# Mirrored score blocks: how they are stored and read back, and when the first expert units' rows are multiplied

## The chip, the cores and the metric

The kernel runs on one core of one Trainium2 chip. The metric is the device time of one execution in microseconds (us). A timed comparison of this kernel can tell a difference of about 0.2% (10 us) from no change.

## The reference, cut to what matters

Eight batches of 3072 tokens go through an attention without softmax, then each token through one of eight experts, then through one dense MLP.

```python
scores = (1 / S) * z @ z.T              # per batch, S = 3072, d_qk = 64: a symmetric matrix
attn   = maximum(scores, 0) ** 2        # symmetric too
x      = u * (attn @ v)                 # v: (3072, 256)
idx    = argmax(norm(x) @ norm(expert_emb).T / tau);  gate = softmax(...)[idx]
x      = gate * (relu(x @ w1[idx]) @ w2[idx])          # 256 -> 1024 -> 256
out    = elu(x @ w_in) @ w_out                         # 256 -> 2048 -> 256
```

All matmuls run in a split form: a factor is cut into a rounded part (hi) and the rest (lo), and hi·hi, hi·lo and lo·hi are summed, three matmuls for one.

## The kernel before

**Attention.** A batch has six chunks `c` of 512 query columns, and each chunk has twelve steps `m`, of 256 key rows each; `k = m // 2` is the 512-row key block. 8 x 6 x 12 = 576 steps make the attention stage. A step has a score part (four matmuls `pss<-zp,zk`, `pss<-zq,zk`) and, two steps later, an accumulating part (`psa<-hi,v`, `psa<-lo,v`, twelve matmuls). ScalarE (ACT) applies ReLU and square, and ACT or VectorE (DVE) make hi and lo.

Since the score matrix is symmetric, block (c, k) with k > c is computed once. In a step that computes it (a calc step), DVE transposes the two halves into a tile `mt` (`mir_tr`), and `mir_put` stores the 1 MB block in the DRAM buffer `mir[b, c, k]`. When the later chunk comes to it (a held step, `m < 2c`), it has no score matmuls: `mir_get` loads a tile `mr` for each step, `mir_g` and `mir_d` make hi and lo of it. Chunk 0 has no held step, chunk 5 has ten of twelve (`order_of` interleaves held and calc steps). A held step is 12 matmuls long and a calc step 16.

**Behind a chunk** `evac_ops` multiplies the sum with u, transposes it (`xt`) and stores it in the DRAM buffer `xr`. Behind each pair of chunks `pair_ops` loads the rows back (`x<-xr`, function `get`), ACT squares them with a row sum (line 617, `sq`), and `route_ops` computes gates and positions; POOL scatters token numbers into `tok`, eight scatters per pair, each behind the one before.

**Experts and MLP.** After the attention, units follow: A (512 rows of one expert), B (256 rows), M and D (MLP on 512 rows). For A and B, POOL gathers token numbers (`ids`), rows (`rows<-xr,ids`) and weights (`wst`); DVE multiplies the rows by their gate (line 1013's `gates`), SP stores them in `xg` (`put`) and loads them back in transposed order (`xt<-xg`, `get`).

**Order of the work.** All instructions are issued in program order on each engine, and this order is written out by hand: `at(n, fn)` hangs a piece of work on step n, `spread` shares pieces over a range of steps by planned loads of ACT and DVE. SP issues nearly all plain DMAs, in order, and waits in order: a DMA whose data or buffer isn't ready holds up all DMAs behind it. POOL does the same for gathers and scatters.

**Buffers.** Nearly all SBUF tiles come from one pool of 4 KB-per-partition slots (tag `g`, `NSLOT` = 45); `mt` and the gathered `rows` share a second pool (tag `wide`, `NWIDE` = 2). A new tile waits for the last user of the slot that it gets.

Steps that the change touches, with n the step of use: `mir_get` at n - `AHEAD` (line 1344); `mir_put` two steps after the second half (line 1353); for a pair that ends at step w, `get` at w + 3 and `sq` from w + `EV` + 3 (lines 1462 and 1465), the routing from w + `EV` + 9; for the first two expert units (units 0 and 1, at steps 576 and 580) gathers at n - 32 and n - 27, gates and `put` at n - 25 and n - 20, read-back at n - 15 and n - 10 (lines 1513 to 1543).

Of the kernel before, what the change touches and what calls it, by code (L numbers as in the profile page):

```python
# [7 lines left out]
F32 = mybir.dt.float32  # L8
F32R = mybir.dt.float32r
# [6 lines left out]

LAG = 2
RL = 5
EV = 4
NSLOT = 45  # L20
NWIDE = 2
AHEAD = 8


def ceil_div(a, b):
# [4 lines left out]
def attn_moe_mlp(ctx, tc, zT, zK, uT, v, emb, embT, tau, wp, w_in, w_out, out):  # L30
# [25 lines left out]
    XW = D + 64  # L56
# [8 lines left out]
    mir = {(b, c, k): dr.tile([128, 2048], F32, name="mir")  # L65
           for b in range(B) for c in range(NC) for k in range(c + 1, NC)}
# [3 lines left out]
    def again(tag):  # L70
        q = fixed[tag]
        q.append(q.pop(0))
        return q[-1]

    def slot(name, dt=F32, shape=(2, 512)):
        if fixed:
            w = 1
            for s_ in shape:
                w *= s_
            t = again("gr" if dt == F32R else "g")[:, :w]  # L80
            if len(shape) == 1:
                return t
            names = "abcd"[:len(shape)]
            return t.rearrange("p (%s) -> p %s" % (" ".join(names), " ".join(names)), **dict(zip(names[1:], shape[1:])))
        return sb.tile([128] + list(shape), dt, name=name, tag="g", bufs=NSLOT)

    def rslot(name):
        return slot(name, F32R)

    def wide(name, shape):  # L90
        if fixed:
            return again("wide")
        return sb.tile([128] + shape, F32, name=name, tag="wide", bufs=NWIDE)

# [16 lines left out]
    vec, act, pool, pe, sp = nc.vector, nc.scalar, nc.gpsimd, nc.tensor, nc.sync  # L111
# [46 lines left out]
    def at(n, fn, s=0):  # L158
        tasks[n][s].append(fn)
# [187 lines left out]
    P, PK, Q, V, XS, UT, AC, HL, PS, MT = {}, {}, {}, {}, {}, {}, {}, {}, {}, {}  # L347
# [124 lines left out]
    def mir_tr(C, m):  # L472
        k, s_ = divmod(m, 2)

        def fn():
            if s_ == 0:
                MT[C, k] = wide("mt", [8, 2, 2, 2, 32])
            vec.transpose(out=MT[C, k][:, :, s_], in_=MT.pop((C, k, s_)).rearrange("p j (x q r) -> p x q j r", q=2, r=32))
        return fn

    def mir_put(C, k):
        b, c = divmod(C, NC)

        def fn():
            sp.dma_start(mir[b, c, k], MT.pop((C, k)).rearrange("p x s q j r -> p (x s q j r)"))
        return fn

    def mir_get(C, m):
        b, c = divmod(C, NC)
        k, s_ = divmod(m, 2)  # L490

        def fn():
            t = HL[C, m] = slot("mr", F32, (4, 256))
            src = mir[b, k, c].rearrange("(i r) f -> r i f", r=32)
            for q in range(4):
                o = (q * 2 + s_) * 256
                sp.dma_start(t[q * 32:(q + 1) * 32], src[:, :, o:o + 256])
        return fn

    def x8(t):  # L500
        return t.rearrange("p j (x y) -> p j x y", y=64)

    def mir_g(C, m, n):
        r = HL[C, m].rearrange("p i (s j y) -> p j (i s) y", j=2, y=64)
        hi = rslot("hi")
        on_act = use_act(n, 1.15)
        if on_act:
            cp(x8(hi), r)
        HL[C, m] = hi, r, on_act
# [828 lines left out]
    for C in range(NCH):  # L1338
        c = C % NC
        for m in order_of(c):  # L1340
            n = len(steps)
            steps.append((held if m < 2 * c else calc, (C, m, n)))
            if m < 2 * c:
                at(n - AHEAD, mir_get(C, m))
                loadA[n] += 0.9
                loadD[n + 1] += 2.1
            else:
                loadA[n] += 2.0
                loadD[n + 1] += 1.2
                if m // 2 > c:  # L1350
                    at(n + 1, mir_tr(C, m), -1)
                    if m % 2:
                        at(n + 2, mir_put(C, m // 2))
                    loadD[n + 2] += 1.25

    units = [("A", 0)]
# [3 lines left out]
    j, t = NA1, 0  # L1360
# [68 lines left out]
    for b in range(B):  # L1429
        for c2 in range(1 if b == 0 else 0, NC // 2):  # L1430
            nat, swap = q_ops(b, c2)
            w = (b * NC + 2 * c2) * CS
            spread([nat], w - 10, w - 9, 0, 1.25)
            at(w - 8, swap)
    for b in range(1, B):
        n0 = (b - 1) * NC * CS
        half = NK // 8
        for k4 in range(half, NK // 4):
            vl, vo = v_ops(b, k4)
            w = n0 + 5 * CS + LAG + 2 * (k4 - half)  # L1440
            at(w - 5, vl)
            pairs(vo, w + 1, w + 3, 0.6, 0.52)
        for c2 in range(NC // 2):
            zl, zo = z_ops(b, c2)
            w = n0 + 4 + c2 * CS
            at(w, zl)
            pairs(zo, w + 4, w + 12, 1.13, 0.95)
        for k4 in range(half):
            vl, vo = v_ops(b, k4)
            w = n0 + CS + 2 + k4 * 8  # L1450
            at(w, vl)
            pairs(vo, w + 3, w + 9, 0.6, 0.52)
    for C in range(NCH):
        at(C * CS + 4, u_load(C))
        w = (C + 1) * CS + LAG
        mul, tr, put = evac_ops(C)
        spread([mul], w - 1, w, 1.2)
        spread([tr], w, w + 1, 1.25)
        at(w + 1, put)
        if C % 2:  # L1460
            dots, get, sq = pair_ops(chunk_group[C][0])
            at(w + 3, get)
            pre[w + 2].append(dots)
            loadD[w + 3] += 0.4
            spread(sq, w + EV + 3, w + EV + 8, 0, 0.55)
    route_end = {}
    late = []
    for g, cs in enumerate(groups):
        seg1, rank, seg2, sc, g5 = route_ops(g)
        w = (cs[-1] + 1) * CS + LAG + EV + 9  # L1470
        L = RL
# [17 lines left out]
    w = route_end[g1]  # L1489
    spread(plan1_ops(), w + 1, w + 6, 0.2)  # L1490
    p1 = w + 6
    w = route_end[len(groups) - 1]
# [6 lines left out]
    for i, (ld, ops) in enumerate(cb):  # L1499
        per = ceil_div(len(cb), B)  # L1500
        w = (i // per) * NC * CS + (i % per + 1) * 2 * CS // per - (CS if i >= per else 0)
# [3 lines left out]
    for un in units:  # L1505
        n = start[un]
        pv = prev[un]
        k = un[0]
        if k in "AB":
            lo_ = p1 if k == "A" and un[1] < NA1 else p2 + 1  # L1510
            wl, w1, w2 = weight_ops(un)
            ro, gates, put, get, h = rows_ops(un)
            w = max(n - (9 if k == "A" else 6), lo_)
            wr = max(n - 9, lo_)
            if un == units[0]:
                w, wr = n - 16, n - 32
                assert wr >= lo_
            if pv is not None and pv[0] == "B" == k:
                assert False
            if pv is not None and pv[0] == "M" and prev[pv] is not None and prev[pv][0] in "AB":  # L1520
                wr = max(n - 16, lo_)
            elif un == units[1]:
                wr = n - 27
            for o in ro:
                at(wr, o, 2)
            for o in wl:
                at(w, o, 2)
            if pv is not None and pv[0] in "AB":
                q = start[pv] + (2 if pv[0] == "A" else 1)
                o = (0, 1, 1, 2, 2, 3)  # L1530
            elif pv is not None:
                q = n - 3
                o = (0, 3, 3, 4, 5, 6)
            else:
                q = max(n - 7, lo_ + 3)
                o = (0, 1, 1, 2, 2, 3)
            for x, o_ in zip((w1[0], w1[1], w2[0], w2[1], w2[2], w2[3]), o):
                pairs(x, q + o_, q + o_ + 1, 0.6, 0.52)
            assert wr + 5 <= n - 4, (un, wr - n)
            early = un in units[:2]  # L1540
            wp_ = wr + 7 if early else max(wr + 3, n - 11)
            at(wp_, lambda gates=gates, put=put: ([g_() for g_ in gates], put()))
            at(wr + 17 if early else max(wr + 5, n - 9), get)
            tr, hl = xt_ops(un, h, XT, 4 if k == "A" else 2)
            spread([tr], n - 4, n - 3, 1.25)
            pre[n - 2] += hl
        elif k == "D":
            dl, do = d_prep(un)
            tr, hl = do
            at(n - 6, dl)  # L1550
            spread([tr], n - 4, n - 3, 1.25)
            pre[n - 2] += hl
        if k in "MD" and un != units[-1]:
            w = n + nst[k] + LAG - 1
            tr, put, get, *sc = out_ops(un)
            at(w, tr)
            at(w + 1, put)
            at(w + 2, get)
            spread(sc, w + 4, w + 6)
# [5 lines left out]

    def rest_tiles():
        with tc.If(count["v"] >= NBS):
            mine = {"g": [slot("rest", F32, (1024,)) for _ in range(5)],
                    "gr": [slot("restr", F32R, (1024,)) for _ in range(12)], "wide": [wide("rows", [4, XW])],
                    "s": [t_ps() for _ in range(2)], "acc": [t_acc()],  # L1570
                    "ids": [sb.tile([128, 4], I32, name="ids", tag="ids", bufs=8)]}
            fixed.update(mine)
            for t in range(NBS, NB):
                un = ("B", t)
                wl, w1, w2 = weight_ops(un)
                ro, gates, put, get, h = rows_ops(un)
                tr, hl = xt_ops(un, h, XT, 2)
                for o in ro + wl + gates + [put] + [o for x in w1 for o in x] + [get] + [o for x in w2 for o in x] + [tr] + hl:
                    o()
                for k in range(2):  # L1580
                    ab_h(un, k)
                    ab_d(un, k)
                for k in range(2):
                    b_acc(un, k)
            fixed.clear()
# [66 lines left out]
```

## Time and profile before

| | us |
|---|---|
| median of three runs | 5135.99 |
| lowest, highest | 5133.37, 5138.31 |
| the profiled execution | 5144.09 |
| its span, first to last instruction | 5142.3 |
| TensorE (PE) busy | 5100.9 (99%) |
| DVE busy | 3997.6 (78%) |
| ACT busy | 3463.5 (67%) |
| POOL busy | 1378.3 (27%) |
| the attention stage, until its last matmul | about 1947 |

The busy times are of one profiled execution. [...] A timeline gives each instruction with its start, its length, and in brackets how long its engine was idle before it and what released it; for SP and POOL it is their queues of DMA issues (SPq, POOLq). A wait for several things is put down to the one that came last by the profile, so the name of a DMA there can be that of another.

### The profile page before, as it was taken

Reading aid. Unit: us, or ns where it says so; the run is one execution under the profiler, and the core shown is the slowest. Engines: PE = TensorE matmul, PEld = TensorE weight load, DVE = VectorE, ACT = ScalarE, POOL = GpSimd, SP = SyncE. Lnnn points to the kernel's source line nnn. Section 1 sums busy time; section 2 is a strip of 40 time slices with the busy share of each in tenths; the row PEclk is TensorE's granted clock in tenths of the full one; section 3 lists DMA queues with packets and bytes.
Section 4 is the critical chain, followed back from the end, with each engine's and each line's share of the span. In section 5 each row is a group of like instructions: output and inputs, shape, how many; then the busy total and the mean of one; then the engine's idle time right before and its main releaser. Section 6 shows DMA issues by size and latency. Waiting matters only on the chain. (4 is left out here: it accounts for less than half of the span.)

```text
span 5142.3 us, 67066 instructions
## 1 busy us (share of the span) xinstructions
PE 5100.9 (99%) x23600; PEld 4234.4 (82%) x23600; DVE 3997.6 (78%) x5099; ACT 3463.5 (67%) x4101; POOL 1378.3 (27%) x1159
## 2 busy tenths in 40 slices
PE   9999999999999999999999999999999999999998
PEld 7788888888888778888888888888888888888887
DVE  8687878787787867887777777777777777777887
ACT  8586767667676755676666666666666666666776
POOL 0011111111111033424444444444333333331011
PEclk9999999999999999999999999999999999999999
DMA  8898879888979695324334334334233333331221
GB/s 248 220 234 194 231 187 233 197 219 211 217 194 223 184 230 154 83 60 124 104 109 127 98 105 130 100 107 131 80 84 84 84 84 84 84 85 50 46 50 38
DMA packets 713109, 708.32 MB, mean 138 GB/s; under 512 B 417916, under 2 KB 622975, under 8 KB 697408
## 3 DMA queue, kind: packets, MB, share of 16 engines
q1 hardware_dynamic: 639296, 500.07, 39.2%
q0 software_dynamic: 73472, 203.91, 13.0%
q8 instruction: 188, 3.08, 0.3%
q14 instruction: 153, 1.25, 0.1%
HBM read 440.20 MB, written 252.04 MB: 135 GB/s over the span
## 5 line engine op out<-in xcount | busy, mean ns | idle before, releaser
L135 PE MATMUL psa<-hi,v 128*128 128x512 f32 x4608 | 1149.6, 392 | 12.9 <-ACT hi L132 6.8
L135 PEld LDWEIGHTS psa<-hi,v 128*128 128x128 f32 x4608 | 864.1, 188 | 203.4 <-ACT hi L132 10.8
L135 PE MATMUL pss<-x2h,wi 128*128 128x512 f32 x2624 | 809.1, 390 | 0.0
L135 PE MATMUL psa<-hi,wo 128*128 128x512 f32 x3008 | 743.3, 389 | 0.0
L124 DVE SCALAR_TENSOR_TENSOR y<-e,y 128x1024 f32<-128x1024 f32 x384 | 467.5, 1218 | 308.7 <-ACT e L1182 307.0
L135 PEld LDWEIGHTS psa<-hi,wo 128*128 128x128 f32 x3008 | 564.7, 188 | 116.8
L1128 ACT ACTIVATE e<-pss 128x1024 f32<-128x1024 f32 x376 | 386.5, 1028 | 404.7 <-PE pss L135 376.7
L744 POOL DMA_INDIRECT tok<-idt,pi x192 | 229.1, 1193 | 1524.4 <-DMA tok<-idt,pi 781.8
L135 PE MATMUL psa<-lo,v 128*128 128x512 f32 x2304 | 617.6, 390 | 4.9 <-DVE lo L114 4.9
L449 ACT ACTIVATE r<-pss 128x1024 f32<-128x1024 f32 x336 | 344.3, 1025 | 393.5 <-PE pss L135 392.5
L1054 ACT ACTIVATE hi<-pss 128x1024 fp32r<-128x1024 f32 x198 | 203.8, 1029 | 571.9 <-PE pss L135 571.9
L135 PEld LDWEIGHTS pss<-x2h,wi 128*128 128x128 f32 x2624 | 490.6, 188 | 99.9
L135 PEld LDWEIGHTS psa<-lo,v 128*128 128x128 f32 x2304 | 433.1, 188 | 96.7 <-DVE lo L114 6.2
L135 PE MATMUL pss<-x2l,wi 128*128 128x512 f32 x1312 | 510.9, 389 | 0.0
L948 POOL DMA_INDIRECT out<-o,ids x192 | 242.4, 1262 | 981.2 <-DMA o<-orow 512.0
L114 DVE TENSOR_TENSOR y<-r,y 128x1024 f32<-128x1024 f32 x384 | 470.6, 1225 | 33.9 <-DVE y L124 1.4
L114 DVE TENSOR_TENSOR lo<-r,hi 128x1024 fp32r<-128x1024 f32 x336 | 408.9, 1217 | 109.3 <-ACT hi L132 106.3
L114 DVE TENSOR_TENSOR lo<-y,hi 128x1024 fp32r<-128x1024 f32 x384 | 470.6, 1226 | 21.6
L1182 ACT ACTIVATE e<-e 128x1024 f32<-128x1024 f32 x384 | 407.8, 1062 | 12.2
L1181 ACT ACTIVATE y<-e 128x1024 f32<-128x1024 f32 x384 | 407.2, 1061 | 9.5
L135 PE MATMUL pss<-xh,w 128*128 128x512 f32 x1312 | 404.7, 390 | 0.9 <-DVE w L114 0.6
L135 PE MATMUL psa<-hi,w 128*128 128x512 f32 x1312 | 405.1, 390 | 0.0
(181 smaller groups left out, 9100.9 us busy)
## 6 DMA issues: line engine op xcount, KB each, us to landing
mir<-mt SPq DMA_DIRECT2D x120, 1024.0 KB, 6.2
mr<-mir SPq DMA_DIRECT2D x960, 128.0 KB, 5.8
vs<-v SPq DMA_DIRECT2D x48, 512.0 KB, 8.4
u<-uT SPq DMA_DIRECT2D x48, 512.0 KB, 6.1
xr<-xt SPq DMA_DIRECT2D x192, 128.0 KB, 3.8
x<-xr SPq DMA_DIRECT2D x96, 256.0 KB, 9.5
orow<-xt SPq DMA_DIRECT2D x188, 128.0 KB, 2.6
o<-orow SPq DMA_DIRECT2D x47, 512.0 KB, 3.9
```

The source lines that it names most:

```text
L114: vec.tensor_tensor(out=o, in0=a, in1=b, op=op)
L124: vec.scalar_tensor_tensor(out=o, in0=a, scalar=s, in1=b, op0=op0, op1=op1)
L135: pe.matmul(o, lhsT=l, rhs=r, start=start, stop=stop, skip_group_check=True, tile_position=pos)
L449: act.activation(out=r, in_=p, func=AF.Relu, scale=1.0 / S)
L744: pool.indirect_dma_start(out=tok[:, :], out_offset=bass.IndirectOffsetOnAxis(ap=h["pi"][:, t:t + 1], axis=0), in_=K["idt"][:, gt:gt + 1], ...
L948: pool.indirect_dma_start(out=dst, out_offset=bass.IndirectOffsetOnAxis(ap=idx, axis=0), in_=src, in_offset=None, bounds_check=bound, oob_ ...
L1054: act.activation(out=hi, in_=p, func=AF.Relu)
L1128: act.activation(out=e, in_=p, func=AF.Relu, scale=-1.0)
L1181: act.activation(out=y, in_=e, func=AF.Tanh, scale=0.5)
L1182: act.activation(out=e, in_=e, func=AF.Exp, scale=-1.0)
```

## The change

The block in DRAM gets another layout. `mt` is arranged so that each partition holds four runs of 512 numbers (2 KB). `mir_put` stores it with four DMAs of 256 KB, each from 32 partitions, two at step n + 2 and two at n + 3, where one DMA of 8 KB runs from all 128 partitions did it. `mir_get` loads a whole block, both steps' halves, with one DMA of 8 KB per partition into all 128 partitions, where eight DMAs (four for each step) of 1 KB runs, each into 32 partitions, did it. The tile that it fills (`mw`) comes from the `wide` pool and no longer from the slots. It is issued five steps ahead of the block's first step, where each half was issued eight ahead.

The pool of slots shrinks from 45 to 39, `wide` grows from 2 to 5. The read-back of x behind a pair moves from w + 3 to w + 5, squares and routing three steps later. For expert units 0 and 1, gathers move to n - 26 and n - 20, gates and `put` to n - 16 and n - 12, the read-back to five steps behind them (n - 11 and n - 7). The number and sizes of matmuls, and what DVE and ACT compute, stay.

```diff
-EV = 4
-NSLOT = 45
-NWIDE = 2
-AHEAD = 8
+EV = 7
+NSLOT = 39
+NWIDE = 5
+AHEAD = 5
...
-                MT[C, k] = wide("mt", [8, 2, 2, 2, 32])
-            vec.transpose(out=MT[C, k][:, :, s_], in_=MT.pop((C, k, s_)).rearrange("p j (x q r) -> p x q j r", q=2, r=32))
+                MT[C, k] = wide("mt", [4, 2, 4, 2, 32])
+            vec.transpose(out=MT[C, k][:, :, s_], in_=MT.pop((C, k, s_)).rearrange("p j (x q r) -> p x q j r", q=4, r=32))
...
-    def mir_put(C, k):
+    def mir_put(C, k, part):
...
-            sp.dma_start(mir[b, c, k], MT.pop((C, k)).rearrange("p x s q j r -> p (x s q j r)"))
+            t = MT[C, k] if part == 0 else MT.pop((C, k))
+            dst = mir[b, c, k].rearrange("(x r) f -> r x f", r=32)
+            for i in (2 * part, 2 * part + 1):
+                sp.dma_start(dst[:, :, i * 512:(i + 1) * 512],
+                             t[i * 32:(i + 1) * 32].rearrange("p x s q j r -> p x (s q j r)"))
...
-    def mir_get(C, m):
+    def mir_get(C, k):
...
-            t = HL[C, m] = slot("mr", F32, (4, 256))
-            src = mir[b, k, c].rearrange("(i r) f -> r i f", r=32)
-            for q in range(4):
-                o = (q * 2 + s_) * 256
-                sp.dma_start(t[q * 32:(q + 1) * 32], src[:, :, o:o + 256])
+            t = wide("mw", [8, 2, 2, 64])
+            sp.dma_start(t.rearrange("p x s j y -> p (x s j y)"), mir[b, k, c])
+            for s_ in range(2):
+                HL[C, 2 * k + s_] = t[:, :, s_]
...
-        r = HL[C, m].rearrange("p i (s j y) -> p j (i s) y", j=2, y=64)
+        r = HL[C, m].rearrange("p x j y -> p j x y")
...
-                at(n - AHEAD, mir_get(C, m))
+                if m % 2 == 0:
+                    at(n - AHEAD, mir_get(C, m // 2))
...
-                        at(n + 2, mir_put(C, m // 2))
+                        at(n + 2, mir_put(C, m // 2, 0))
+                        at(n + 3, mir_put(C, m // 2, 1))
...
-            at(w + 3, get)
+            at(w + 5, get)
...
-                w, wr = n - 16, n - 32
+                w, wr = n - 16, n - 26
...
-                wr = n - 27
+                wr = n - 20
...
-            wp_ = wr + 7 if early else max(wr + 3, n - 11)
+            wp_ = n - (16 if un == units[0] else 12) if early else max(wr + 3, n - 11)
...
-            at(wr + 17 if early else max(wr + 5, n - 9), get)
+            at(wp_ + 5 if early else max(wr + 5, n - 9), get)
...
-            mine = {"g": [slot("rest", F32, (1024,)) for _ in range(5)],
-                    "gr": [slot("restr", F32R, (1024,)) for _ in range(12)], "wide": [wide("rows", [4, XW])],
+            mine = {"g": [slot("rest", F32, (1024,)) for _ in range(4)],
+                    "gr": [slot("restr", F32R, (1024,)) for _ in range(10)], "wide": [wide("rows", [4, XW])],
```

The last two lines belong to a branch for left-over tiles (`rest_tiles`), which these inputs don't take.

## Rows read from the trace of the kernel before

**Rows 1.** The page: busy time of each engine, instructions, issues of the mirrored blocks.
```profile
PE 5100.9 (99%) x23600; PEld 4234.4 (82%) x23600; DVE 3997.6 (78%) x5099; ACT 3463.5 (67%) x4101; POOL 1378.3 (27%) x1159
...
mir<-mt SPq DMA_DIRECT2D x120, 1024.0 KB, 6.2
mr<-mir SPq DMA_DIRECT2D x960, 128.0 KB, 5.8
```
**Rows 2.** View by windows: all stretches of the attention where TensorE loses time.
```profile
230.00:250.00 20.00, 15.96 (x65) 12.61 (x64) 9.04 (x15) 8.15 (x11) 0.00 (x0) 0.91 0.68 180
715.00:725.00 10.00, 8.52 (x38) 6.47 (x37) 4.01 (x6) 5.45 (x6) 0.00 (x0) 1.00 0.52 154
1670.00:1680.00 10.00, 8.23 (x38) 6.23 (x36) 2.84 (x5) 4.36 (x5) 0.00 (x0) 1.00 0.75 197
1835.00:1850.00 15.00, 11.49 (x45) 8.84 (x44) 11.21 (x20) 6.21 (x7) 7.38 (x7) 0.89 0.64 155
1858.00:1868.00 10.00, 8.60 (x37) 6.43 (x36) 9.53 (x23) 5.04 (x5) 7.87 (x8) 1.00 0.73 187
1890.00:1910.00 20.00, 14.65 (x57) 11.67 (x56) 7.12 (x7) 9.06 (x22) 0.00 (x0) 0.83 1.12 271
```
**Rows 3.** Timeline of ACT: two waits, in the first and the last batch.
```profile
236.61 1.06 ACT L132 ACTIVATE hi<-mr 128x1024 fp32r<-128x1024 f32 x1 [11.28 <-DMA xr<-xt]
...
1895.79 0.42 ACT L617 ACTIVATE x<-x 128x256 f32<-128x256 f32 x1 [12.12 <-DMA x<-xr]
```
**Rows 4.** Timeline of DVE: two waits in the last batch.
```profile
1836.89 1.25 DVE L478 STREAM_TRANSPOSE mt<-r 128x1024 f32<-128x1024 f32 x1 [5.21 <-DMA mir<-mt]
...
1857.21 0.35 DVE L118 TENSOR_SCALAR rows<-rows 128x256 f32<-128x256 f32 x1 [6.72 <-DMA rows<-xr,ids]
```
**Rows 5.** Timeline of SP's DMA queue, in the first and the last batch.
```profile
219.46 9.20 SPq L497 DMA_DIRECT2D mr<-mir  x8
...
1827.40 0.34 SPq L485 DMA_DIRECT2D mir<-mt  x1
```
**Rows 6.** Timeline of POOL: scatters of the last pair before unit 0, unit 0's gathers.
```profile
1783.68 1.28 POOL L744 DMA_INDIRECT tok<-idt,pi  x1 [40.18 <-DVE pi L716]
...
1842.68 1.06 POOL L943 DMA_INDIRECT ids<-tok,ixa  x1 [4.86 <-DMA tok<-idt,pi]
...
1855.78 1.00 POOL L943 DMA_INDIRECT rows<-xr,ids  x1 [0.30 <-issue]
```
**Rows 7.** View by windows: mr loads; an mt store; an xt store; an o load.
```profile
1101.50:1103.50 2.00, 2.00 (x11) 1.65 (x10) 2.00 (x3) 1.38 (x4) 0.00 (x0) 1.00 1.35 216
521.00:523.00 2.00, 2.00 (x11) 1.65 (x10) 2.00 (x3) 1.85 (x2) 1.67 (x1) 1.00 1.07 442
...
868.00:870.00 2.00, 2.00 (x11) 1.65 (x10) 2.00 (x2) 0.62 (x1) 1.14 (x2) 1.00 1.02 221
3196.50:3198.50 2.00, 2.00 (x12) 1.69 (x11) 1.43 (x3) 2.00 (x5) 0.00 (x0) 1.00 1.00 351
```
**Rows 8.** View by windows: chunks 1 and 5 of the second batch.
```profile
299.60:340.60 41.00, 41.00 (x184) 33.77 (x183) 38.05 (x67) 36.02 (x39) 4.95 (x5) 1.00 0.93 258
...
456.70:493.10 36.40, 36.40 (x163) 29.98 (x162) 26.32 (x51) 20.41 (x26) 4.07 (x4) 1.00 0.66 148
```
**Rows 9.** The tile `vs` (v as loaded), from 250 to 1800 us: landing of its loads.
```profile
DMA to landing us min/median/max: 7.9/8.4/8.9
```
**Rows 10.** The tile `wst`, from 2100 to 4800 us: landing of its gathers.
```profile
DMA to landing us min/median/max: 4.1/5.1/7.5
```
**Rows 11.** Timelines of POOL, DVE and ACT: a B unit's rows, gates and weights.
```profile
2550.17 1.72 POOL L943 DMA_INDIRECT rows<-xr,ids  x1 [0.30 <-issue]
...
2553.70 1.73 POOL L943 DMA_INDIRECT wst<-wp,wiB  x1 [0.30 <-DVE w L114]
...
2558.26 0.61 DVE L118 TENSOR_SCALAR rows<-rows 128x256 f32<-128x256 f32 x2
...
2576.68 1.66 ACT L132 ACTIVATE w<-wst 128x512 fp32r<-128x512 f32 x3
```

## The prediction before the run

> **What bounds the kernel now.** I read the page first: TensorE is busy 99% of the span [rows 1], so the kernel is a queue of matmuls and only stretches in which TensorE stands still can give anything. The change leaves every matmul in place, so the second view is the one by windows, searched for stretches in which TensorE's busy time is short of the window. In the attention stage there are six [rows 2]; idle time in them is 4.04, 1.48, 1.77, 3.51, 1.40 and 5.35 us, 17.6 us together. [...] Counted as lost clock that is 0.09 x 20 + 0.11 x 15 + 0.17 x 20 = 6.9 us, an upper bound since part of it falls into the idle time itself. So **at most 24.4 us (0.5%)** can be won; the first microseconds, the tail and the expert stage have losses that the change doesn't touch.
>
> The third view says what each stretch waited for. At 230, ACT wanted an `mr` tile for 11.28 us [rows 3], and its loads had been issued slowly, eight of them in 9.20 us [rows 5]: the loads of mirrored blocks had fallen behind. The name in the bracket is of another DMA. The stretches at 715 and 1670 look the same; all three lie in the last chunk of a batch, where ten of twelve steps read mirrored blocks. At 1835, DVE waited 5.21 us before a transposition into `mt` [rows 4]: one of the two `wide` buffers held unit 0's gathered rows, and the other was still being stored by the DMA issued at 1827.40 [rows 5]. At 1858, DVE stood 6.72 us before unit 0's gate products because the rows had not landed [rows 4]. At 1890, ACT stood 12.12 us before the squares of x [rows 3].
>
> **The change, part by part.**
>
> *Five `wide` buffers.* The 5.21 us wait needs both buffers taken. With at most three to four `mt` and `mw` tiles alive at once in a batch (a block is held about eight steps from its load to its last use, and one comes every 2.4 steps in chunk 5), the wait goes. In the last batch the rows of a unit make it five of five, so there SP may wait for the buffer of a `mir_get`, with u's and x's DMAs queued behind it; that stays inside the five steps of lead. Gain 3.51 + 1.65 = 5.2 us.
>
> *Gates of units 0 and 1 later.* DVE reached unit 0's gates at 1857.21 - 6.72 = 1850.5 [rows 4]; they move nine steps later, 9 x 3.0 us (a chunk of 36.4 us has twelve steps [rows 8]) = 27 us, less the 5.2 us just won: 1872. The rows depend on POOL, which was busy with eight scatters from 1783.68 until the gathers at 1842.68 [rows 6]. The routing comes three steps later, so this chain and the gathers behind it come up to 9 us later: the last rows, 1857.2 before, at 1866. The margin is 6 us. Gates and the `put` that waits for them on SP then hold up nobody. Unit 1 moves by eight steps and has the same margin or more; its read-back keeps three steps, 9 us, before it is transposed. Gain 1.4 us.
>
> *x later.* Squares move three steps, their load two, which alone is 3 us against a wait of 12.12. What matters more is SP's order: the load stood behind unit 0's `put`, itself waiting for the gates until 1857; now it stands ahead of that `put`. The routing that follows is late by 9 us, and only units 0 to 5 can feel that, through POOL. Gain 5.35 + 3.4 us at most; I take 7.5.
>
> *Mirrored blocks read whole.* Per block, eight loads into 32 partitions become one. Loads of `mr` move 216 GB/s, a DMA of 8 KB runs over 128 partitions 442 [rows 7]: 1 MB in 4.85 or 2.4 us. SP issues 120 loads, not 960 [rows 1], and the eight issues of 9.20 us become one like that of `mir<-mt`, 0.34 us [rows 5]. In chunk 5, with five blocks, that takes 12 us off DMA engines that are busy 0.66 x 36.4 = 24 us in a quiet batch [rows 8]. The lead shrinks from eight steps to five, 15 us in chunk 5; the 1 MB store took 6.2 us from issue to landing [rows 1], so some 9 us are to spare. Gain: 5.8 us at 230 and 3.2 at 715 and 1670, of which I take 7.5.
>
> *Stores from 32 partitions.* This is the price, and no row shows this form. Its bounds: 351 GB/s, the 1 KB loads into 128 partitions, so 3.0 us a block, or 216 to 221 GB/s [rows 7], so 4.8. The rows divide by partitions and not by length of run: with 1 KB runs it is 216 into 32 partitions and 351 into 128, and the `xr<-xt` store from 32 partitions has 221. I take 4.8: a store then costs 2.4 us more, as much as a read saves, and the DMA load of a batch stays what it was but moves from its last chunks to its first. In chunk 1, with some five blocks stored and one or two read, 0.93 x 41.0 = 38.1 us of DMA [rows 8] become 38.1 + 5 x 2.4 - 1.5 x 2.4 = 46.5, which is 5.5 us too much for 41.0; chunk 3 and later give it back. At the other bound it is 38.1 + 3 - 3.6 = 37.5 us. Queued behind are v (loaded three or more steps of 3.4 us ahead, landing in 8.4 us [rows 9]) and the reads themselves (five steps, 17 us). Five microseconds of lateness are covered for the reads, and for v by its first use, mostly five steps after its issue. I cost it at nothing.
>
> [...]
>
> *Six slots fewer.* In the attention this pays for `mr`, up to eight of which were alive by the order of the steps. In the expert stage, 3.2 ms, it is a loss. A step of the MLP takes five slots (`e`, `y`, `r`, `hi`, `lo`) and lasts 24 matmuls, some 5.4 us, so a slot comes free 6/5 of a step later, 6.5 us. POOL's weight gathers feel it first. Their lead is 2576.68 - 2553.70 = 23 us [rows 11] and they land in at most 7.5 [rows 10], so 9 us stay. Behind them on POOL wait the next rows, the tightest 2558.26 - 2550.17 = 8.1 us before their gates [rows 11]; 6.5 us later, with 1.72 of issue and about 4 to landing, DVE would wait some 4 us in a few of 17 B units. Bounds: nothing, or those 4 us in all 17 less about 2 us of DVE's lead each, 34 us. I take nothing: most units have more lead, and the slot used next is not always the last one freed.
>
> **Sum.** 5.2 + 1.4 + 7.5 + 7.5 = 21.6, say **21 us**. The profiled execution took 5144.09 us, so it would take 5123; the median lies 8.1 us (0.16%) under it, so the forecast is **5115 us** (0.4% faster). If everything in the six windows goes, it is 5112; the standstills of the timed runs may be shorter or longer than those profiled, hence down to 5106.
>
> **The rivals.**
>
> *Stores clog the first chunks (slower).* At 216 GB/s chunk 1 ends 5.5 us late. If v and the reads of chunk 2 then miss their steps, ACT, which works in order, stands before v's conversion, and TensorE behind it, in each of eight batches. Price: 5.5 us x 8 = 44 on top of the forecast: **5159**. For it: the 0.93 [rows 8]. Against it: DMA shares count overlapping packets, and x's load now comes behind v's. It decides once the lateness passes some 5 us.
>
> *Fewer slots delay POOL (no change).* The 34 us bound halved, 17 us, against 21 won: **5132**, within 0.2%.
>
> *The standstills only move (no change).* Five steps of lead instead of eight, with DMAs as late as 11 us at times [rows 3], let the reads come late elsewhere, and the hand-over to the experts waits for POOL's chain. Only the two `wide` and gate parts stay, 7 us: **5129**.
>
> **How the numbers follow.** Forecast 0.70, stores 0.10, slots 0.08, moved standstills 0.12. A comparison tells about 0.2% (10 us) from no change, so below 5125.7 is faster and above 5146 slower. Faster: 0.70 and a little of the slots' case, 0.72; slower: the stores' 0.10 and the slots' bad end, 0.12; the rest 0.16. The range 5106 to 5138 covers the forecast, both no-change cases and leaves out the stores' case and the ends. The forecast's own range is 5106 to 5125.
>
> **What would show it.** Right: windows at 230, 715, 1670, 1835, 1858 and 1890 full at clock 1.00; `mw` loads landing in about 6 us and some 9 us before use; stores of 256 KB moving near 217 GB/s; DMA share of chunk 5 lower and of chunk 1 higher. Wrong: ACT idle before `v` or `hi<-mw` in chunks 1 to 3, DVE idle before `rows` in the B units, or SP waiting for `wide` buffers so long that the next read is late.

## The result, and the profile after

The change made the kernel slower: 5200.93 us (median of four runs, 5199.93 to 5213.47) against 5134.68 for the kernel before beside it (5132.61 to 5138.31). The ratio is 1.0133, with a 95% interval of 1.0121 to 1.0145. The forecast was 5115, so it missed by 86 us and had the wrong sign.

The profiled execution of after has a span of 5211.7 us, 69.4 more than that of before (it is the longest of the four runs; the medians differ by 66.2). First I cut both spans where the attention stage ends, at the start of its last matmul `psa<-lo,v`. The stage ends at 1946.7 us before and at 1989.9 after, 43.2 later. The expert stage behind it takes 3195.6 and 3221.8 us, 26.2 more. So there are two losses, in two stages, and neither lies where the forecast had looked for one.

The answer to [rows 1], from the page of after. The four stores and the one load per block are there as written, and TensorE has lost a point of its share:

```profile
PE 5126.4 (98%) x23600; PEld 4240.6 (81%) x23600; DVE 3976.9 (76%) x5078; ACT 3481.8 (67%) x4122; POOL 1340.7 (26%) x1159
...
mir<-mt SPq DMA_DIRECT2D x480, 256.0 KB
mw<-mir SPq DMA_DIRECT2D x120, 1024.0 KB
```

The six windows of [rows 2], in the trace of after (busy time of PE, PEld, DVE, ACT and POOL with their counts, the clock granted to TensorE as a share of full speed, the mean busy share of the DMA engines, which is over 1 where packets overlap, and GB/s):

```profile
230.00:250.00 20.00, 13.96 (x58) 11.19 (x57) 7.58 (x18) 5.49 (x7) 4.12 (x5) 0.92 0.37 81
715.00:725.00 10.00, 10.00 (x46) 8.29 (x45) 8.77 (x14) 9.51 (x16) 0.98 (x1) 1.00 0.82 252
1670.00:1680.00 10.00, 10.00 (x56) 7.58 (x55) 8.79 (x20) 5.04 (x5) 0.00 (x0) 1.00 0.70 210
1835.00:1850.00 15.00, 15.00 (x79) 12.02 (x72) 14.17 (x28) 8.29 (x10) 1.04 (x1) 1.00 0.86 221
1858.00:1868.00 10.00, 10.00 (x46) 8.29 (x45) 5.62 (x15) 7.26 (x12) 1.50 (x1) 1.00 1.02 306
1890.00:1910.00 20.00, 16.01 (x67) 12.58 (x67) 10.74 (x23) 7.33 (x8) 7.94 (x8) 0.89 0.75 190
```

Four are full. The windows lie at the same times as before, while the same work comes later here, so it takes the list of PE's waits to say what is left. The first and the last window still have a hole, but the DMA engines are quieter there (0.37 where it was 0.68, 0.75 where it was 1.12). It is another hole, and the waits of PE up to 1950 us name it:

```profile
PE pss L135 <- DMA zq<-zp: 47.3, 13, 6.0
PE pss L135 <- ACT zk L132: 6.2, 1, 6.2
```

Thirteen times TensorE stood before a score matmul because its tile `zq` had not landed, 47.3 us in all; before, this line does not exist. `zq` is the copy of `zp` with its halves of 64 partitions exchanged. It is made by two DMAs on **POOL's** queue, hung on step w - 8, eight steps before a pair of chunks starts (`swap` in `q_ops`). One such place, first in PE's timeline, then by windows:

```profile
909.21 0.39 PE L135 MATMUL pss<-zp,zk 128*128 128x512 f32 x1
914.48 0.77 PE L135 MATMUL pss<-zq,zk 128*128 128x512 f32 x1 [4.88 <-DMA zq<-zp]
```

```profile
911.00:916.00 5.00, 1.52 (x5) 0.94 (x6) 0.00 (x0) 0.00 (x0) 0.00 (x0) 0.63 0.42 79
916.00:922.00 6.00, 6.00 (x23) 4.83 (x23) 1.77 (x3) 5.04 (x5) 0.00 (x0) 0.74 0.00 0
```

The second window is the price on top: after a standstill of 4.88 us TensorE runs on at a granted clock of 0.74 in this window. Taken apart by smaller windows it is 0.50 from 912.4 to 919.1 us and 1.00 from 919.2 on. What kept the copies is in POOL's timeline, here of after, then the same place of before, with PE's first matmul on that `zq` below it:

```profile
853.50 1.04 POOL L746 DMA_INDIRECT tok<-idt,pi  x1 [46.51 <-DVE sm L129]
862.37 1.01 POOL L746 DMA_INDIRECT tok<-idt,pi  x1 [7.83 <-DMA tok<-idt,pi]
...
904.22 0.98 POOL L746 DMA_INDIRECT tok<-idt,pi  x1 [6.97 <-DMA tok<-idt,pi]
905.19 0.59 POOL L409 DMA_DIRECT2D zq<-zp  x1
```

```profile
821.66 1.05 POOL L744 DMA_INDIRECT tok<-idt,pi  x1 [27.80 <-DVE pi L716]
...
868.86 0.98 POOL L744 DMA_INDIRECT tok<-idt,pi  x1 [2.77 <-DMA mr<-mir]
869.83 0.59 POOL L409 DMA_DIRECT2D zq<-zp  x1
```

```profile
895.51 0.39 PE L135 MATMUL pss<-zq,zk 128*128 128x512 f32 x1
```

Both queues are the same: eight scatters of a pair's token numbers, each waiting for the one before to land, and right behind the last one the copies. Before, they were issued at 869.83 and land in a median of 8.0 us, about 878; TensorE's first matmul on that `zq` started at 895.51, so some 17 us were to spare. After, the scatters start 31.8 us later than the 821.66 of before (13.9 us of it because the kernel was already that late), the copies leave at 905.19, and TensorE wants them at 909.4.

In the expert stage no single line is large. One place of it, after the change, on POOL, then ACT, then PE:

```profile
2580.64 0.98 POOL L950 DMA_INDIRECT dn<-xo,dpB  x1 [0.30 <-ACT y L1183]
2588.84 1.25 POOL L950 DMA_INDIRECT dnid<-ids,dpB  x1 [7.22 <-DMA dnid<-ids,dpB]
2590.39 1.03 POOL L950 DMA_INDIRECT dn<-xo,dpB  x1 [0.30 <-issue]
```

```profile
2599.57 1.06 ACT L1183 ACTIVATE y<-e 128x1024 f32<-128x1024 f32 x1 [6.16 <-DMA dn<-xo,dpB]
```

```profile
2602.68 0.73 PE L135 MATMUL pss<-x2h,wi 128*128 128x512 f32 x2 [2.18 <-ACT r L1115]
```

ACT computes `y` from its own `e`; it has no business with `dn<-xo`. It waits because the slot that its `y` gets was that of `xo`, and POOL's second scatter out of `xo` has just left. Behind `y` on ACT stands the ReLU `r` that empties TensorE's score buffer, and TensorE waits 2.18 us. With fewer slots in the ring, a new tile meets a user that isn't done. From 2100 to 3700 us ACT's `y` waits 51.5 us for such scatters, in 12 places; before, never.

### The profile page after: what moved, and what is told of

The parts are those of the page before. It is cut to its first block, busy times and chain, and to the rows that moved or that the text cites. A ratio compares the mean times of both kernels' runs of the same rounds, so it can differ in the third digit from the quotient of the medians.

```text
span 5211.7 us, 66339 instructions
## 1 busy us (share of the span) xinstructions
PE 5126.4 (98%) x23600; PEld 4240.6 (81%) x23600; DVE 3976.9 (76%) x5078; ACT 3481.8 (67%) x4122; POOL 1340.7 (26%) x1159
## 3 DMA queue, kind: packets, MB, share of 16 engines
q0 software_dynamic: 73472, 203.91, 12.7%
## 5 line engine op out<-in xcount | busy, mean ns | idle before, releaser
L135 PE MATMUL psa<-hi,v 128*128 128x512 f32 x4608 | 1157.3, 394 | 0.0
L135 PEld LDWEIGHTS psa<-hi,v 128*128 128x128 f32 x4608 | 869.9, 190 | 190.5 <-issue 6.2
L135 PE MATMUL pss<-x2h,wi 128*128 128x512 f32 x2624 | 811.3, 390 | 9.9 <-ACT r L1115 9.6
L135 PE MATMUL psa<-hi,wo 128*128 128x512 f32 x3008 | 744.5, 390 | 1.3 <-issue 0.5
L135 PEld LDWEIGHTS psa<-hi,wo 128*128 128x128 f32 x3008 | 563.5, 188 | 122.3 <-issue 4.2
L135 PE MATMUL psa<-lo,v 128*128 128x512 f32 x2304 | 617.6, 390 | 0.0
L135 PEld LDWEIGHTS pss<-x2h,wi 128*128 128x128 f32 x2624 | 490.2, 188 | 114.0 <-ACT r L1115 13.5
L135 PE MATMUL pss<-x2l,wi 128*128 128x512 f32 x1312 | 511.0, 389 | 0.0
L135 PEld LDWEIGHTS psa<-lo,v 128*128 128x128 f32 x2304 | 434.4, 189 | 91.6
L950 POOL DMA_INDIRECT out<-o,ids x192 | 231.3, 1205 | 906.3 <-DMA o<-orow 454.4
L1183 ACT ACTIVATE y<-e 128x1024 f32<-128x1024 f32 x384 | 407.4, 1061 | 83.8 <-DMA dn<-xo,dpB 51.5
L135 PE MATMUL pss<-xh,w 128*128 128x512 f32 x1312 | 408.5, 391 | 4.2 <-DVE w L114 2.2
L135 PE MATMUL psa<-hi,w 128*128 128x512 f32 x1312 | 404.9, 390 | 0.0
```

The costliest lines, as they stand in the source:

```text
L135: pe.matmul(o, lhsT=l, rhs=r, start=start, stop=stop, skip_group_check=True, tile_position=pos)
L950: pool.indirect_dma_start(out=dst, out_offset=bass.IndirectOffsetOnAxis(ap=idx, axis=0), in_=src, in_offset=None, bounds_check=bound, oob_ ...
L1183: act.activation(out=y, in_=e, func=AF.Tanh, scale=0.5)
```

## The experiments

Three theories had to be told apart. **Theory 1**: the routing three steps later puts the scatters ahead of the `zq` copies. **Theory 2**: 39 slots instead of 45 cost the expert stage its 26 us. Against them: the new mirror transfers make things late, or the first units' new steps do. **Theory 3**, on the gains: the parts of the change bring what the sum gave them. All runs, with the cut of the profiled span as above (the kernel before took 5134.6, 5136.8, 5136.8 and 5132.4 us beside the runs of e1 to e4, e5 to e8, e9 to e11 and e12):

| kernel | attention ends at | rest of the span | median us | ratio to before, 95% |
|---|---|---|---|---|
| before | 1946.7 | 3195.6 | 5134.68 | 1 |
| after | 1989.9 | 3221.8 | 5200.93 | 1.0121 to 1.0145 |
| e1 after, `zq` copies on SP | 1924.3 | 3216.7 | 5142.27 | 1.0004 to 1.0023 |
| e2 after, routing back | 1921.1 | 3221.1 | 5142.70 | 1.0002 to 1.0021 |
| e3 before, routing later | 2022.3 | 3193.4 | 5222.16 | 1.0153 to 1.0187 |
| e4 before, six slots held | 1942.7 | 3215.0 | 5159.49 | 1.0027 to 1.0055 |
| e5 e2 + `x2h`, `x2l` in `wide` | 1921.0 | 3222.3 | 5145.44 | 1.0008 to 1.0027 |
| e6 e5 + `xo` in `wide` | 1921.1 | 3222.4 | 5145.43 | 1.0008 to 1.0027 |
| e7 e2 + first gates back | 1922.1 | 3217.9 | 5145.49 | 1.0006 to 1.0025 |
| e8 before + later gates, x | 1971.7 | 3195.3 | 5162.89 | 1.0029 to 1.0063 |
| e9 e5, as two tiles | 1921.4 | 3222.4 | 5145.48 | 1.0007 to 1.0027 |
| e10 e3 + copies on SP | 1941.1 | 3192.5 | 5137.60 | 0.9992 to 1.0011 |
| e11 e2 + DMA tiles in `wide` | 1921.1 | 3195.0 | 5117.72 | 0.9948 to 0.9976 |
| e12 e2 + `xh`, `xl` in `wide` | 1921.1 | 3236.2 | 5158.40 | 1.0029 to 1.0062 |

### e1: the copies past POOL's queue

```
-            pool.dma_start(q[0:64], p[64:128])
-            pool.dma_start(q[64:128], p[0:64])
+            sp.dma_start(f(q[0:64]), f(p[64:128]))
+            sp.dma_start(f(q[64:128]), f(p[0:64]))
```

> The changed kernel, with the two copies that make each zq tile issued by SP's queue in place of POOL's. Theory 1 (routing three steps later puts its eight POOL scatters, 46 us, ahead of the zq copies in POOL's queue; TensorE waits for zq at 13 places, about 65 us with the clock's ramp behind them): PE's waits for zq go, the attention stage ends about 65 us sooner, at about 1925 us, and the kernel takes about 5136 us. Rival 1 (the new 8 KB mirror loads and 2 KB stores make the copies themselves late): the waits stay and the kernel takes 5190 to 5205 us. The expert stage keeps its 26 us loss by either.

5142.27 us; the attention stage ends 65.6 us sooner, at 1924.3. What waits for the tile `zq` is ACT's ReLU alone, which comes after the matmuls anyway; PE and PEld are gone from the list, which for after said "PEld pss L135: 52.4, 13" and "PE pss L135: 47.3, 13":

```profile
who waited for it (us, times):
  ACT r L449: 428.9, 254
  ACT zk L132: 0.8, 1
```

Theory 1 holds to within a microsecond of its 65, and rival 1 falls: the mirror transfers are all still there.

### e2: the routing back

```
-EV = 7
+EV = 4
-            at(w + 5, get)
+            at(w + 3, get)
```

> The changed kernel with only EV 7 -> 4 and the read-back of x at step w+5 -> w+3, as before the change; mirror stores, mirror loads, five wide buffers, 39 slots and the later first gates stay. Theory 1: PE's waits for zq go, some 60 us less (up to 9 us may come back at the end of the attention stage, where x is read again earlier): 5133 to 5145 us. Rival 1 (mirror transfers delay zq): 5190 to 5205 us.

5142.70 us, and the attention stage ends at 1921.1, 68.8 us sooner than after and 25.6 sooner than before. Here every one of the six windows is full at clock 1.00, and the last of PE's waits up to 1950 us is over at 42 us; before has six behind that time that are longer than a microsecond. The two losses are now clear of each other: the `zq` waits took 68.8 us of the attention, and the gain of the change came beside them, 25.6 us. That gain is one profile against another. The profiled run of before took 5144.09 us, 7 to 12 more than the medians beside the experiments, and e4, whose attention stage has the same instructions as that of before, ends it at 1942.7. By the medians the gain is about 18 us (see e11). The possible 9 us for x at the old steps did not come back: ACT waits 4.6 us for x in 2 places, where it waited 26.8 us in 11 before.

### e3: the routing alone

```
-EV = 4
+EV = 7
-            at(w + 3, get)
+            at(w + 5, get)
```

> The kernel before with only EV 4 -> 7 and the read-back of x at step w+3 -> w+5. Theory 1: the zq waits come to a kernel that has none of the other parts: 45 to 65 us more than before, 5180 to 5200 us, with PE waiting for zq at steps 48 and 72 of the batches. Rival 1: no such waits, 5125 to 5140 us.

5222.16 us: the kernel before with nothing but this is slower than after. The waits of PE, up to 1950 us:

```profile
PE pss L135 <- DMA zq<-zp: 58.1, 10, 10.9
PE psa L135 <- DVE hi L533: 8.6, 2, 8.3
```

The sign and the place were right; 88 us is more than the 45 to 65 expected, since the copies come later still (922.60 at the place where after has 905.19, with 12.5 us of the difference from delays ahead of it).

### e4: six slots held

```
+    hold = []
+    def take():
+        for _ in range(6):
+            t = slot("held")
+            vec.memset(t[:, 0, :1], 0.0)
+            hold.append(t)
...
+    at(start["A", 6], take)
+    at(start["M", 38], give)
```

> The kernel before with six of its 45 slots taken by idle dummy tiles from the first step of expert unit A6 to the first step of M38; nothing else differs, six memsets and copies of one column are added. Theory 2 (39 slots in place of 45 cost the expert stage its 26 us): the expert stage is 15 to 26 us longer, the kernel takes 5150 to 5161 us, and ACT waits for y behind the scatters of dn. Rival 2 (the expert stage lost its time to its first units alone, or to another part of the change): 5132 to 5140 us.

5159.49 us; the expert stage is 19.4 us longer, and the waits from 2100 to 3700 us have the line of after (51.5 us there):

```profile
ACT y L1181 <- DMA dn<-xo,dpB: 50.1, 12, 5.8
```

Theory 2 holds: six slots fewer, and nothing else, cost about three quarters of the loss by the profiles, and 24.9 us by the medians; the dummies are held for a part of the stage only.

### e5, e6 and e9: the slots given back, and a new price

The five `wide` buffers have little to do in the expert stage. e5 takes the two factors of an M unit's first layer from there (e9 the same as two tiles, e6 with `xo` besides):

```
-                    X2[key] = rslot("x2h"), rslot("x2l")
+                    x2 = wide("x2", [2, 2, 512], F32R)
+                    X2[key] = x2[:, 0], x2[:, 1]
```

> The run with routing back (changed kernel with EV 4 and x read at w+3), and the pair x2h, x2l of each A unit taken as one 8 KB tile from the five wide buffers, which only the rows gathers use in the expert stage. Theory 2a (the 39 slots go round in order, and the x2 pairs, held from the end of an A unit to the end of its M unit, are what a new tile has to wait for): the expert stage goes from 3221 us back to 3195 to 3205, the kernel takes 5118 to 5128 us. Rival 2b (the slots of xo, held by POOL's slow scatters, are what ACT's y waits for): the x2 pairs change little, 5136 to 5143 us, and ACT's waits for y behind dn stay at about 50 us.

> As e5, and xo of the B units from the wide buffers as well. Theory 2a: no more than 5 us less than e5. Rival 2b: this alone brings the expert stage back, to about 3195 us and the kernel to 5115 to 5122 us; ACT's waits for y behind dn go.

5145.44 and 5145.43 us: nothing won, and neither range of e5 holds. Rival 2b, which comes nearest, is not the reason, since its waits, ACT's `y` behind `dn`, are gone in both. Compared unit by unit with before, e5 falls behind by a steady 0.62 to 0.75 us in each of the 41 M units (not 37, as two of the expectations have it), up to the end of the kernel, where e2 loses in steps of 1 to 5 us and only until 3700 us. The views by line and form show it, from 3950 to 4700 us, where slots are no matter; first e5, then before. The tile `x2` is printed as `x` there, and the number behind the busy time is the mean ns of one matmul:

```profile
L135 PE MATMUL pss<-x,wi 128*128 128x512 f32 x1106 | 269.8, 393 | 0.0
L135 PE MATMUL psa<-hi,wo 128*128 128x512 f32 x738 | 185.1, 393 | 0.0
...
L135 PE MATMUL pss<-xh,w 128*128 128x512 f32 x352 | 108.4, 389 | 0.0
```

```profile
L135 PE MATMUL pss<-x2h,wi 128*128 128x512 f32 x751 | 231.4, 389 | 0.0
L135 PE MATMUL psa<-hi,wo 128*128 128x512 f32 x744 | 183.8, 389 | 0.0
```

The matmuls are the same, but their starts lie 230.4 ns apart on average instead of 226.6, so that a step of an M unit takes 5.53 us instead of 5.44 in the timeline of PE. Was it the merged tile?

> As e5, but x2h and x2l each as a tile of its own in the five wide buffers (half of each buffer stays unused). In e5 the waits for slots went, but every matmul started in the steps of an M unit came 230.4 ns after the one before on average, with 226.6 in the run with routing back, some 0.65 us for each of 37 M units, which took back what the slots gave. Theory 4a (it is the shape: both tiles in one): 226.7 ns again, the expert stage at 3195 to 3200 us, the kernel at 5116 to 5122 us. Theory 4b (it is the place: the moving operand read from the wide buffers): 230 ns stays, the kernel at 5140 to 5146 us.

5145.48 us, where e5 took 5145.44, and an expert stage of 3222.4 us, where e5's is 3222.3: it is not the shape. Of the two theories that leaves 4b, the place.

### e12: another operand in the same place

```
-                dst[key] = rslot("xh"), rslot("xl")
+                dst[key] = wide("xh", [2, 512], F32R), wide("xl", [2, 512], F32R)
```

> The run with routing back, and xh, xl of the A and D units (the moving operand of an A unit's first layer) as two tiles from the wide buffers; x2h and x2l stay in the slots. Theory 4b (a moving operand read from the wide buffers slows the matmuls of its steps): now the matmuls started in the steps of A units come about 230 ns apart and those of M units 226.7 ns; 37 A units of four steps lose some 0.35 us each, 13 us, while the slots gain up to 25: 5125 to 5145 us. Theory 4c (it is the other work of an M unit that slowed the matmuls in e5, e6 and e9): 226.7 ns in A and M units alike, and with the slots' gain 5116 to 5130 us.

The same view of e12 has the slow matmuls in the A units now, and M's first layer as fast as ever:

```profile
L135 PE MATMUL pss<-x2h,wi 128*128 128x512 f32 x746 | 229.6, 389 | 0.0
...
L135 PE MATMUL pss<-xh,w 128*128 128x512 f32 x352 | 109.7, 393 | 0.0
```

So 4b holds for a second operand; it costs 15 us in 41 A units and 4 us in the D units, which have such tiles too. The time, 5158.40 us, is outside what either theory gave, because most of the slots' loss stayed, some 22 of the 40.6 us (ACT's `y` waits 53.0 us behind `dn`): to give these two tiles another place relieves little.

### e11: only tiles that TensorE doesn't read

```
-            x = slot("xo", F32, (4, 256))
+            x = slot("xo", F32, (4, 256)) if fixed else wide("xo", [4, 256])
...
-            h["o"] = slot("o", F32, (4, 256))
+            h["o"] = wide("o", [4, 256])
...
-            h["t"] = slot("xt", F32, (16, 2, 32))
+            h["t"] = slot("xt", F32, (16, 2, 32)) if fixed else wide("xt", [16, 2, 32])
```

(`fixed` belongs to the branch for left-over tiles, which these inputs don't take.)

> The run with routing back, and the tiles of the expert stage that only DMA, ACT and DVE touch (xo, the output tile o, and the xt tile of the x read-back) from the five wide buffers; x2h and x2l stay in the slots. Theory 2 (slots): the expert stage comes back to 3195 to 3205 us without a slower matmul, the kernel takes 5116 to 5126 us. Rival (six tiles of a unit pair through five wide buffers wait for each other, and the rows gathers with them): 5135 to 5160 us, with POOL's rows late.

5117.72 us (5117.44 to 5117.88), faster than before at a ratio of 0.9962 (0.9948 to 0.9976), and the fastest kernel of this study: 19.0 us by the medians, 26.2 by the profiled spans. The expert stage is back at 3195.0 us, so all but 0.6 us of that is the attention's. PE's waits over its whole span begin so:

```profile
PE pss L135 <- ACT zk L132: 6.4, 1, 6.4
PE pss L135 <- ACTq L1571: 1.6, 1, 1.6
```

The first is the start of the kernel; ACTq is ACT's instruction sequencer. Nothing is left in the attention, and with the slots relieved and the matmuls at a mean of 389 ns from 3950 to 4700 us, as before has them, almost nothing in the experts (before has the same waits there): theory 2 once more. Which of the three tiles does it was not tried.

### e7, e8 and e10: whose gains they were

e7 is e2 with the first units' steps as before, so only the mirror layout, the single read and the five buffers are left of the attention's part:

```
-                w, wr = n - 16, n - 26
+                w, wr = n - 16, n - 32
...
-            at(wp_ + 5 if early else max(wr + 5, n - 9), get)
+            at(wr + 17 if early else max(wr + 5, n - 9), get)
```

> The run with routing back, and the gate products, the row gathers and the x read-back of the first two expert units where they stood before the change: so of the change's attention part only the mirror layout, the single read and the five wide buffers are left. The prediction's sum gives the later gates 1.4 us and the later x 7.5: by it the attention stage ends about 1.4 us later than with routing back (1921.1), or up to 9 us later if x belongs to this as well. Rival 3 (the mirror parts bring back all of it by themselves): 1921 to 1922 us again, the kernel the same within 3 us.

The attention stage ends at 1922.1: the mirror parts alone bring 24.6 of the 25.6 us, and the later gates 1.0, where the sum said 1.4. So small a difference can be read here: six profiles with the attention stage of e2 (e2, e5, e6, e9, e11, e12) end it at 1921.0 to 1921.4. Rival 3 holds.

e8 is the kernel before with the later gates and the x read-back at w + 5, EV 4 as it was:

> The kernel before with only the x read-back two steps later (w+3 -> w+5) and the first two units' gathers, gates and read-back later; EV stays 4, mirrors, slots and wide buffers are as before. The prediction's sum: 9 us less (x 7.5, gates 1.4): the attention stage ends at about 1938 us and the kernel takes about 5126 us. Rival 3 (x and v were late because the mirrored transfers ahead of them were, and the steps do nothing alone): the stage ends at 1945 to 1947 us, the kernel takes 5132 to 5136 us.

25 us slower in the attention stage, against both theories. The edit was a poor one: it moves the read-back of x without its use, which hangs on EV, and leaves it two steps. ACT, in order, waits for it:

```profile
ACT x L617 <- DMA x<-xr: 128.5, 16, 15.0
```

e10 does it properly, five steps between the two, and the copies on SP so that POOL's queue is no matter (the edits of e3 and e1 on the kernel before):

> The kernel before with EV 4 -> 7, the x read-back at w+3 -> w+5, and the two zq copies on SP's queue: the change's later x with five steps between read-back and use, without the zq waits and without the mirror parts. The prediction's sum gives the later x 7.5 us: the attention stage ends at about 1939 us, the kernel takes about 5127 us. Rival 3 (the mirror parts alone bring back the standstills): 1943 to 1948 us, 5131 to 5137 us. Theory 1 asks that the zq waits are gone by either: a stage end beyond 1960 us speaks against it.

No `zq` wait, and a stage end at 1941.1, 5.6 us sooner than before; by the time no difference (0.9992 to 1.0011). Before and e4, with the same instructions in that stage, already end it 4.0 us apart, so the 5.6 us are not shown to be a gain. The window at 1890 is full, but its standstill has only moved behind it. It is as long as it was, 5.37 us where it was 5.35, and ACT stands before a weight tile of the experts instead of before x; here PE, then ACT:

```profile
1924.53 2.08 PE L135 MATMUL psa<-hi,v 128*128 128x512 f32 x4 [5.37 <-DVE hi L533]
```

```profile
1921.12 0.63 ACT L132 ACTIVATE w<-wst 128x512 fp32r<-128x512 f32 x1 [8.80 <-DMA xr<-xt]
```

The window at 230 still has 2.4 us of standstill, and that at 1835 a granted clock of 0.89. So x later, without the mirror parts, cured none of the three longest standstills; with the mirror parts all three are gone, and x stands at its old steps there (e2, e7).

Not tried: the mirror parts one by one (the stores, the single read, the five buffers). Which of them brings the 24.6 us is open.

## Why the prediction was wrong, by its own steps

**What bounds the kernel** was read rightly. At most 24.4 us were to be had in the six windows; e2 won 25.6 in that stage, measured against the same profile. The 6.9 us in it for a lower clock are read from [rows 2], 1 less 0.91, 0.89 and 0.83 times each window. Smaller windows of the same trace put it at the three longest standstills: the granted clock is 0.50 from 237.7 to 241.1, 1842.0 to 1845.3 and 1896.6 to 1903.3 us, 13.4 us together, which counts as 6.7.

**The sum's 21 us** were there to be had, 25.6 by the profiles and about 18 by the medians, but not where it put them. By the profiles the mirror parts, 12.7 in the sum, brought 24.6; the gates 1.0 instead of 1.4; x nothing instead of 7.5, and alone (e10) no time either. Each window had been given to one part by the wait that came last in it, and e7 shows that the mirror parts end nearly all of them. That this is one cause upstream, SP's queue full of mirrored loads, fits that but is not shown, since the mirror parts were not taken apart.

**The step that failed** is half a sentence in *x later*: "The routing that follows is late by 9 us, and only units 0 to 5 can feel that, through POOL." The routing runs behind every pair of chunks, not only behind the last. Behind each pair's scatters the next thing in POOL's queue is the copies of `zq` for the pair of chunks that comes, 21 times, and 13 of them came too late. The prediction looked at POOL only where the attention ends [rows 6], and it did not list what POOL's queue holds. The rows for it were there: the scatters, hung on eight consecutive steps of 3.4 us, wait for one another and take 1842.68 - 4.86 - 1783.68 = 54 us [rows 6], twice what their steps allow. Started at step 4 of the 24 of a pair they were through at about step 18, the copies two steps late, with 17 us to spare. At the place shown they start 17.9 us later against the matmuls (31.8 by the clock, less the 13.9 that the kernel was late), and that uses up all of it. EV was taken as a delay of three steps, 9 us; in POOL's queue it was twice that. From the first square of x to the result that the scatters wait for (`pi`) it takes 64.5 us there, where it took 57.6. The price of it all was 68.8 us.

**Six slots fewer** was a term of the sum taken at nothing with bounds of nothing and 34 us. It is 26 (after) and 19 to 25 (e4, by profiles and by medians), inside the bounds and in their upper half. The place was wrong too: not the gathered rows ahead of DVE, but ACT behind `xo`, a tile that POOL's scatters hold. The reasoning followed POOL's gathers, the tiles that are taken early, and did not ask which tile is *released* late.

**Stores from 32 partitions** were priced at 4.8 us a block, from the slow end of [rows 7]. For two of them alone that about holds: when only the first two stores of a block are out, from partitions 0 to 31 and 32 to 63, they move 196 GB/s together. In a place where SP issues all four in a row, the block moves at 401 GB/s for 2 us. SP's queue of after, the place with two stores first, then the windows:

```profile
353.19 0.78 SPq L488 DMA_DIRECT2D mir<-mt  x2
...
883.49 3.47 SPq L488 DMA_DIRECT2D mir<-mt  x4
```

```profile
354.50:356.50 2.00, 2.00 (x11) 1.64 (x10) 1.93 (x5) 0.36 (x1) 0.00 (x0) 1.00 0.99 196
886.00:888.00 2.00, 2.00 (x11) 1.65 (x10) 0.00 (x0) 1.97 (x2) 0.00 (x0) 1.00 1.05 401
...
302.60:343.60 41.00, 41.00 (x184) 33.75 (x183) 38.00 (x60) 36.56 (x49) 4.08 (x5) 1.00 0.97 276
464.90:503.20 38.30, 36.81 (x164) 29.94 (x163) 24.48 (x44) 22.52 (x31) 6.95 (x7) 1.00 0.45 140
```

The last two lines answer [rows 8]. Chunk 1 of the second batch has 0.97 x 41.0 = 39.8 us of DMA, not 46.5; put into the prediction's own formula (38.1 + 5 x (p - 2.4) - 3.6) that is p = 3.5 us a block, an estimate that lies nearer to the lower bound of 3.0 than to 4.8. The prediction's mark for the stores, near 217 GB/s, lies between the 216 and the 221 of [rows 7]; two stores stay under it and four move almost twice as much, and why is not shown by these runs. That the stores cost TensorE nothing was right all the same: chunk 5 went from 0.66 to 0.45, and ACT waited 6.5 us in 4 places for `mw` in the whole kernel.

**From the profile to the median.** The prediction took 8.1 us off because the median lies that much under the profiled run, after it had taken the profile's standstills off. That counts something twice. e11 has none of them, and its runs lie within 0.5 us of each other while those of before spread over 5128 to 5145. So by these runs it is the standstills themselves that differ from run to run. Without the 8.1 the six windows gone would have been 5144.1 - 24.4 = 5119.7; e11 took 5117.7.

**The rivals.** Clogging stores did not happen. The slots' case was real but too small. The standstills did not move in the changed kernel; later x alone (e10) did move one. The case that happened, a second queue in the way, was not among them; the sum of 12% for slower was put on the wrong mechanism.

## What to carry to other kernels

A step that is moved takes with it everything that follows from it, in every batch. Write down, for each queue that works in order, what stands behind the moved piece and how long its users can wait; a chain of transfers that wait for each other lasts by its landings, not by the steps it is hung on (54 us here, on eight steps of 3.4). When buffers are taken from a ring, look for the tile that is released last, not for the one that is wanted first; and a part of a change that loses can be undone alone, as e11 shows: 83 us between two versions of the same idea.

## What was not expected of the hardware

The rate of the matmuls changed with the buffers in which their streamed operand lay. With `x2h`, `x2l` in the `wide` buffers (e5), starts of 128x512 matmuls in M's steps came 230.4 ns apart on average, 5.53 us for the 24 of a step, where before they came 226.6 ns apart, 5.44 us; their mean length was 393 ns and not 389. With `xh`, `xl` there (e12), the first layer's matmuls in A's steps, `pss<-xh,w`, had 393 ns where before has 389. Matmuls of the second layer, which read nothing from `wide`, were slower too: `psa<-hi,wo` took 393 ns in e5 where it took 389, `psa<-hi,w` 391 in e12 where it took 389. e6 and e9, with the operands of e5 in the same buffers, took the time of e5 (5145.43 and 5145.48 us against 5145.44); e11, with other tiles in these buffers, has every group of matmuls at 389 ns from 3950 to 4700 us. Why is open: addresses were not varied by themselves.
